# Depthwise causal convolution before a gated MLP: tokens at block edges from a ninth block of each unit, in place of products across blocks

## The chip, the cores and the metric

The kernel runs on one core of a Trainium2 chip. The metric is the device time of one execution in microseconds (us). The kernel before took 734.95 us, the median of three runs (734.82 to 735.59).

The core's engines are named as the profile names them: PE (matrix products, with its weight loads listed apart as PEld), DVE (vector), ACT (scalar and table functions), POOL (general) and SP (here it only issues DMAs and small order-keeping instructions).

## The reference, cut to what matters

`x` is 8 sequences of 4096 tokens with 192 channels in float32. The channels are 8 heads of 24, and each head has 7 taps, made a probability by a softmax:

```python
w = softmax(weight)                                # (8 heads, 7 taps)
y[b, s] = sum over k of w[h, k] * x[b, s + k - 6]  # per head, zeros before a sequence's start
h = y.reshape(32768, 192) @ w_in                   # (192, 2048)
out = (h * cos(h)) @ w_out                         # (2048, 192), float32
```

An output token thus needs itself and the six tokens before it.

## The kernel before, in words

**Units, blocks and tiles.** Tokens are cut into 32 units of 1024, a unit into 8 blocks of 128 tokens with the token on the partition. The MLP works on 64 tiles of 512 tokens, two to a unit.

**The convolution of a unit.** `load_unit` (L66) brings `x` in float32 on SP's queue. `cast_unit` (L163) turns it to bf16 on POOL in three instructions (L176 to L178), which also swap the two row halves of every odd head, and L172 copies the last block of the unit before into a slot ahead of block 0. `conv_mm` (L183) multiplies a block of one head by a banded 128x128 matrix of the taps (`band`); a second banded matrix (`prev`) brings in the last six tokens of the block before. Each product is done on one half of PE's rows (64 of 128), so that two products run side by side. `conv_part` (L210) does four heads: 12 products of 64 rows by 192 columns, six in the step called c1 and six in the step c2. Its two PSUM banks are then cast to bf16 by two ACT copies (`conv_out`, L201, the step called ec). A unit takes two such parts, one in each tile.

**Turning.** `double_unit` (L244, POOL) writes each 64-wide piece twice, and `turn_unit` (L250) sends the unit through a DMA transpose to `cT`, with channels on the partitions.

**The MLP.** A step h0 to h7 (`mm1`, L328) is six products of 64 rows by 512 columns into a PSUM tile `h`. ACT then takes the cosine (L334, as a sine) and DVE multiplies it with `h` to give `g` (L338); the multiply is the last reader of `h`. `h` has three buffers, taken in turn; in a tile the convolution's part takes one too, so the order is h0, conv, h1, h2, ... h7, and h2 gets the buffer of h0. A step "m8" (`mm2_step`, L358) is eight steps of two products of 64 rows by 192 columns, for the tiles before. `evac` (L370, ACT) takes its sums out of PSUM, `store` (L373) writes them.

**What sets the order.** It is written out by hand, once for PE and once for ACT:

```python
PE_ORDER = "h0 c1 m8 c2 h1 m8 h2 h3 m16 | h4 h5 m8 h6 m12 h7 m12"
ACT_ORDER = "P s0 ec s1 s2 s3 Q s4 s5 s6 s7"
PE_FIRST = ["h0 h1 h2 h3 h4 d1 h5 d2 h6 c1 h7 c2 |", "h0 m8 h1 m8 h2 h3 m16 | h4 c1 h5 m8 c2 h6 m12 h7 m12"]
```

s0 to s7 are the sines of h0 to h7 (each with DVE's multiply after it), P and Q the two `evac` copies. At h1 of even tiles POOL is given `double_unit`; at "|" SP is given the transpose (even tiles), the store and the next load (odd tiles), and POOL the cast of the unit after next (even tiles). Tiles 0 and 1 have orders of their own, and tile 0 does two parts (d1, d2 and c1, c2). Tiles 61 to 63 have no convolution, since unit 31 is the last.

`Turn` (L147) makes an empty instruction on SP wait for a product and a later product wait for SP, so that two row halves don't write one bank at a time. Such instructions stand in SP's queue between the DMAs.

Unit 0 is done ahead of the loop by `conv_first` (L278), on all 128 rows and with `prev` products, and turned in part by PE itself (`turn_first`, L288).

Of the kernel before, what the change touches and what calls it, by code (L numbers as in the profile page):

```python
# [8 lines left out]
FP32 = mybir.dt.float32  # L9
BF16 = mybir.dt.bfloat16  # L10
# [6 lines left out]
def kernel(  # L17
# [8 lines left out]
    nc = tc.nc  # L26
    B, S, D = x.shape
    H, K = weight.shape
    Dff = moe_w_in.shape[1]
    G = D // H  # L30
# [4 lines left out]
    U = 1024  # L35
    NU = NTOK // U
    UB = U // 128
    UPS = S // U
# [3 lines left out]
    NC = D // 64  # L42
    R = G // NC

    xf = x.rearrange("b s d -> (b s) d")

    consts = ctx.enter_context(tc.tile_pool(name="consts", bufs=1))
    xin = ctx.enter_context(tc.tile_pool(name="xin", bufs=2))
# [14 lines left out]

    x_tiles = {}

    def load_unit(u, n0=0, n1=UB):  # L66
        if n0 == 0:
            x_tiles[u] = xin.tile([128, UB, D], FP32, name="x_f")
        nc.sync.dma_start(out=x_tiles[u][:, n0:n1, :],
                          in_=xf[u * U + n0 * 128 : u * U + n1 * 128, :].rearrange("(n p) d -> p n d", p=128))  # L70

# [14 lines left out]
    def load_wo(q):  # L86
        for i in range(2):
            nc.sync.dma_start(out=wo_f[:, q * HP : (q + 1) * HP, i], in_=wo_src[:, q * HP : (q + 1) * HP, i])

    load_wo(0)  # L90


# [22 lines left out]
    E = 32 + K - 1  # L115
# [44 lines left out]

    bf = {}

    def cast_unit(u, n0=0, n1=UB):  # L163
        copy = nc.scalar.copy if u == 0 and n0 == 0 else nc.gpsimd.tensor_copy
        if u == 0:
            bf[u] = xb0
        else:
            bf[u] = xbf_pool.tile([128, UB + 1, D], BF16, name="x_bf")
            if u % UPS == 0:
                nc.gpsimd.memset(bf[u][:, 0, :], 0.0)  # L170
            else:
                nc.gpsimd.tensor_copy(out=bf[u][:, 0, :], in_=bf[u - 1][:, UB, :])  # L172

        o = bf[u][:, n0 + 1 : n1 + 1, :].rearrange("p n (h t k r) -> t p (n h) k r", t=2, k=NC, r=R)
        i = x_tiles[u][:, n0:n1, :].rearrange("p n (h t r k) -> t p (n h) k r", t=2, k=NC, r=R)
        copy(out=o[0], in_=i[0])  # L176
        copy(out=o[1, 0:64], in_=i[1, 64:128])  # L177
        copy(out=o[1, 64:128], in_=i[1, 0:64])  # L178
        bf.pop(u - 2, None)

    ct_tiles = {}

    def conv_mm(u, c, ps, i, rows, prev, n0, n1, **flags):  # L183

        h = 4 * c + i
        return nc.tensor.matmul(  # L186
            out=ps[i // 2][:, 0 : (n1 - n0) * 2 * G].rearrange("p (n k i r) -> p i n k r", n=n1 - n0, k=NC, i=2)[:, i % 2],
            lhsT=band[rows, h, 128 if prev else 0 : 256 if prev else 128],
            rhs=bf[u][rows, n0 + 1 - prev : n1 + 1 - prev, h * G : (h + 1) * G].rearrange("p n (k r) -> p n k r", k=NC),
            skip_group_check=True, **flags)  # L190

    def conv_out(u, c, ps, n0, m0, m1, copy, double=False):

        for b in range(2):
            w0 = (2 * c + b) * 2 * R
            o = ct_tiles[u][:, m0:m1, :, :, w0 : w0 + 2 * R].rearrange("p n k t w -> p (n k) t w")
            i = ps[b][:, (m0 - n0) * 2 * G : (m1 - n0) * 2 * G].rearrange("p (m t w) -> p m t w", t=1, w=2 * R)
            if double:
                copy(o, i.to_broadcast([128, (m1 - m0) * NC, 2, 2 * R]))  # L199
            else:  # L200
                copy(o[:, :, 0, :], i[:, :, 0, :])  # L201
# [8 lines left out]
    def conv_part(u, c, banks):  # L210


        ps = banks()
        sides = [slice(0, 64), slice(64, 128)]

        def mm(i, rows, prev=0, **flags):
            return conv_mm(u, c, ps, i, sides[rows], prev, 0, UB, **{"start": False, "stop": False, **flags})


        mm(0, 0, start=True)  # L220
        mm(2, 1, start=True)
        mm(1, 0)
        mm(2, 1, 1)
        m = mm(1, 0, 1)
        turn = Turn()
        turn.mark(m, mm(3, 1))
        yield
        m = mm(2, 0)
        turn.wait(m, mm(0, 1))
        mm(3, 0)  # L230
        mm(0, 1, 1)
        mm(3, 0, 1, stop=True)
        mm(1, 1, stop=True)
        yield
        if c == 0 and u not in ct_tiles:
            ct_tiles[u] = ct_pool.tile([128, UB, NC, 2, 64], BF16, name="ct")
        conv_out(u, c, ps, 0, 0, UB, nc.scalar.copy)
        yield

    cT = {}  # L240

    def double_unit(u, n0=0, n1=UB):
        ct = ct_tiles[u]
        nc.gpsimd.tensor_copy(out=ct[:, n0:n1, :, 1, :], in_=ct[:, n0:n1, :, 0, :])  # L244

    def turn_unit(u, n0=0, n1=UB):
        ct = ct_tiles.pop(u)
        if u not in cT:
            cT[u] = cT_pool.tile([128, UB, NC, 128], BF16, name="cT")
        nc.sync.dma_start_transpose(out=cT[u][:, n0:n1].rearrange("p n c k -> p (n c) k"),  # L250
                                    in_=ct[:, n0:n1].rearrange("p n c t k -> p (n c t k)"))
        cT.pop(u - 2, None)


    cast_unit(0, 0, NB)
# [4 lines left out]
    for d, n, m in ((0, 3, 3), (0, 1, 1), (2, 1, 4), (0, 1, 2)):  # L260
        nc.vector.tensor_tensor(out=prod[:, d : d + n], in0=prod[:, d : d + n], in1=prod[:, d + m : d + m + n], op=ALU.add)


    three = [nc.vector.tensor_copy, nc.scalar.copy, nc.gpsimd.tensor_copy]
    for odd in range(2):
        for q in range(4):
            e0 = 32 * (q ^ (2 * odd))
            three[(4 * odd + q) % 3](out=band[32 * q : 32 * q + 32, odd:H:2, e0 : e0 + E],
                                     in_=prod[32 * q : 32 * q + 32, 0, odd:H:2, :])
    cast_unit(0, NB, UB)  # L270
    for k in range(NC):
        three[(k + 2) % 3](out=w[:, k, 0:HP], in_=w_f[:, k, 0:HP])

    ct_tiles[0] = ct_pool.tile([128, UB, NC, 2, 64], BF16, name="ct")
    cT[0] = cT_pool.tile([128, UB, NC, 128], BF16, name="cT")
    copies = [nc.scalar.copy, nc.vector.tensor_copy]

    def conv_first(n0, n1):  # L278
        for c in range(2):
            ps = ring_banks()  # L280
            for i in range(4):
                for prev in range(2):
                    conv_mm(0, c, ps, i, slice(0, 128), prev, n0, n1, start=prev == 0 and i % 2 == 0, stop=prev == 1)
            yield
            for half in range(2):
                conv_out(0, c, ps, n0, n0 + 2 * half, n0 + 2 * half + 2, copies[half], double=n0 == 0)
# [25 lines left out]
    for q in range(2):  # L312
        nc.gpsimd.tensor_copy(out=wo[:, q * HP : (q + 1) * HP], in_=wo_f[:, q * HP : (q + 1) * HP])  # L313
    load_unit(2)


    g_tiles = {}
# [68 lines left out]
    for t in range(NT + 2):  # L386
        u, second = divmod(t, TPU)
        cu, cc = (u + 2, 0) if second else (u + 1, 1)
        conv = {"c": conv_part(cu, cc, ring_banks if t else o_banks) if cu < NU else iter(())}
        if t == 0:  # L390
            conv["d"] = conv_part(1, 0, o_banks)
        act, done, h, step = (ACT_ORDER if t > 1 else ACT_FIRST[t]).split(), set(), {}, 0

        def flush():
            while act:
                k = act[0]
                need = {"P": "start", "Q": "|", "e": k[1:] + "2"}.get(k[0], "h" + k[1:])
                if need not in done:
                    return
                act.pop(0)  # L400
                if k == "P" and 0 <= t - 2 < NT:
                    evac(t - 2, 0)
                    if t == NT + 1:
                        store(t - 2, 0, 1)
                elif k == "Q" and 0 <= t - 2 < NT:
                    evac(t - 2, 1)
                elif k[0] == "e":
                    next(conv[k[1]], None)
                elif k[0] == "s" and t < NT:
                    gcu(t, int(k[1:]), h.pop(int(k[1:])))  # L410

        done.add("start")
        flush()
        for k in (PE_ORDER if t > 1 else PE_FIRST[t]).split():
            if k[0] == "h" and t < NT:
                h[int(k[1:])] = mm1(t, int(k[1:]))
            elif k[0] in conv:
                next(conv[k[0]], None)
            elif k[0] == "m":
                for q in range(step, step + int(k[1:])):  # L420
                    mm2_step(t, q)
                step += int(k[1:])
            done.add(k)
            flush()

            if k == ("|" if t == 0 else "h1") and second == 0 and cu < NU:
                double_unit(cu)
            if k == "|":
                if second == 0 and cu < NU:
                    turn_unit(cu)  # L430
                if 0 <= t - 2 < NT:
                    store(t - 2, 1 if t == NT + 1 else 0)
                if second == 1 and u + 3 < NU:
                    load_unit(u + 3)
                if second == 0 and u + 2 < NU:
                    cast_unit(u + 2)


# [28 lines left out]
```

## Time and profile before

| | |
|---|---|
| profiled execution | 734.92 us |
| its span, first to last instruction | 733.1 us, so 1.82 us lie around it |
| granted PE clock | 0.999 |
| PE busy | 723.0 us, 99% |
| PEld busy | 554.6 us, 76% |
| DVE busy | 620.0 us, 85% |
| ACT busy | 626.9 us, 86% |
| POOL busy | 177.5 us, 24% |
| the convolution's 64-row products (L186, 192 columns) | 744, 243 ns each as recorded |
| the multiply (L338) | 512, 1221 ns each |
| the sine (L334) | 512, 1025 ns each |

The profile lists instructions by line, engine and shape, with their mean time. A product's recorded time contains its way through PE, so products overlap and their sum is no time of PE; what PE needs for a step is read from the distance between the starts of steps. The chain of waits goes back from the last instruction; each of its pieces is followed to what released it, or to the instruction before it on the same engine.

### The profile page before, as it was taken

To read this page: it belongs to the slowest core of one execution; us is meant where nothing else is said; L and a number is where in the kernel's file an instruction comes from. 1 tells how busy PE (TensorE), PEld (TensorE's weight loads), DVE (VectorE), ACT (ScalarE), POOL (GpSimd) and SP (SyncE) were. 2 spreads that over 40 slices of the span, in tenths; PEclk is the share of its full clock that TensorE was granted. 3 is DMA by queue.
4 is the path that set the end of the run, shared out by engine and by line. 5 is a ranking of instruction groups with operands and counts; after the bars stand their busy time and mean duration, and the time that the engine had idled before them with its cause. 6 is when DMAs were issued, how large, how long until landed. Compare 5 with 4: busy or idle time off the path is not lost.

```text
span 733.1 us, 26791 instructions
## 1 busy us (share of the span) xinstructions
PE 723.0 (99%) x12083; PEld 554.6 (76%) x12083; DVE 620.0 (85%) x538; ACT 626.9 (86%) x785; POOL 177.5 (24%) x177
## 2 busy tenths in 40 slices
PE   7899999999999999999999999999999999999997
PEld 3577777777777777777777777777777777777776
DVE  6888888888888888888888888888888888888883
ACT  6888888888888988988888888888888888888883
POOL 5522211222211222211222211222201222202000
PEclk9999999999999999999999999999999999999999
DMA  9624424434335455334334334344334355353302
GB/s 223 187 68 131 109 89 131 106 92 132 105 92 132 97 100 131 99 99 131 92 105 132 92 106 131 87 111 131 86 112 132 82 116 116 93 120 88 86 27 66
DMA packets 167956, 79.97 MB, mean 109 GB/s; under 512 B 99490, under 2 KB 167074, under 8 KB 167842
## 3 DMA queue, kind: packets, MB, share of 16 engines
q1 hardware_dynamic: 167840, 78.26, 40.8%
q8 instruction: 94, 1.54, 0.9%
q14 instruction: 20, 0.16, 0.1%
q10 hardware_dynamic: 2, 0.00, 0.0%
HBM read 28.31 MB, written 25.17 MB: 73 GB/s over the span
## 4 chain that ended last, share of the span: by engine, by line
PE 98%; DVE 1%; ACT 1%; issue 0%
PE o_ps L358 46%; PE h L328 45%; PE h L186 4%; PE o_ps L101 1%; PE h L358 1%; DVE g L338 1%; ACT cs L334 0%; ACT ct L201 0%; PE o_ps L186 0%; DVE cT L296 0%; ACT o_sb L370 0%; PE h L292 0%; PE o_ps L108 0%; ACT ct L199 0%; DVE ct L199 0%
## 5 line engine op out<-in xcount | busy, mean ns | idle before, releaser
L338 DVE TENSOR_TENSOR g<-h,cs 128x1024 bf16<-128x1024 f32 x512 | 609.1, 1221 | 97.4 <-ACT cs L334 88.8
L334 ACT ACTIVATE cs<-h 128x1024 bf16<-128x1024 f32 x512 | 511.5, 1025 | 78.4 <-PE h L328 77.1
L358 PEld LDWEIGHTS <-g 64*128 64x128 bf16 x8192 | 362.0, 94 | 67.8 <-issue 1.2
L328 PE MATMUL h<-cT,w 64*128 64x512 bf16 x3072 | 401.3, 376 | 2.7 <-DVE g L338 1.4
L358 PE MATMUL o_ps<-wo,g 64*128 64x192 bf16 x8064 | 403.3, 243 | 0.6 <-ACT ct L201 0.6
L328 PEld LDWEIGHTS <-w 64*128 64x128 bf16 x3072 | 166.1, 94 | 84.9 <-issue 3.0
L244 POOL COPY ct<-ct 128x1536 bf16<-128x1536 bf16 (+1 forms) x32 | 46.2, 1444 | 493.1 <-issue 489.6
L370 ACT COPY o_sb<-o_ps 128x384 f32<-128x384 f32 x126 | 60.4, 479 | 5.1 <-PE o_ps L358 2.4
L201 ACT CAST ct<-h 128x384 bf16<-128x384 f32 (+1 forms) x124 | 52.4, 474 | 9.5 <-PE h L186 5.5
L186 PE MATMUL h<-x_bf,band 64*128 64x192 bf16 (+1 forms) x752 | 53.4, 241 | 0.8 <-POOL x_bf L178 0.6
L186 PEld LDWEIGHTS <-band 64*128 64x128 bf16 (+1 forms) x776 | 38.2, 94 | 14.9 <-issue 1.3
L177 POOL CAST x_bf<-x_f 64x768 bf16<-64x768 f32 (+1 forms) x32 | 38.7, 1208 | 2.0
L178 POOL CAST x_bf<-x_f 64x768 bf16<-64x768 f32 (+1 forms) x32 | 38.6, 1206 | 1.9
L176 POOL CAST x_bf<-x_f 128x768 bf16<-128x768 f32 (+1 forms) x32 | 38.8, 1213 | 0.1
L101 PE MATMUL o_ps<-zero 128*128 128x512 bf16 x29 | 9.3, 489 | 1.3 <-DVE zero L96 1.3
L358 PE MATMUL h<-wo,g 64*128 64x192 bf16 x128 | 8.7, 243 | 0.6 <-ACT o_sb L370 0.6
L172 POOL COPY x_bf<-x_bf 128x192 bf16<-128x192 bf16 x24 | 8.3, 344 | 0.0
L101 PEld LDWEIGHTS <-zero 128*128 128x128 bf16 x29 | 3.2, 118 | 6.1 <-issue 3.0
L370 ACT COPY o_sb<-h 128x384 f32<-128x384 f32 x2 | 1.0, 480 | 5.2 <-PE h L358 5.2
L313 POOL CAST wo<-wo_f 128x1536 bf16<-128x1536 f32 x2 | 2.9, 1466 | 0.9 <-DMA wo_f<-in_moe_w_out_dram 0.8
L186 PE MATMUL o_ps<-x_bf,band 64*128 64x192 bf16 x24 | 2.1, 243 | 0.5 <-ACT ct L201 0.3
L258 DVE TENSOR_TENSOR prod<-mask,wn 128x2128 bf16<-128x2128 bf16 x1 | 2.4, 2376 | 0.1
(45 smaller groups left out, 29.3 us busy)
## 6 DMA issues: line engine op xcount, KB each, us to landing
out_dram<-o_sb SPq DMA_DIRECT2D x63, 384.0 KB, 2.9
x_f<-in_x_dram SPq DMA_DIRECT2D x31, 768.0 KB, 5.2
w_f<-in_moe_w_in_dram SPq DMA_DIRECT2D x4, 384.0 KB, 7.8
wo_f<-in_moe_w_out_dram SPq DMA_DIRECT2D x4, 384.0 KB, 4.9
x_f<-in_x_dram SPq DMA_DIRECT2D x2, 384.0 KB, 4.0
cT<-ct SPq DMA_TRANSPOSE x32, 4.6
out_dram<-o_sb SPq DMA_DIRECT2D x2, 192.0 KB, 1.9
w_row<-in_weight_dram ACTq DMA_DIRECT2D x1, 0.2 KB
```

The lines of the kernel that those rows point to most:

```text
L101: nc.tensor.matmul(out=idle, lhsT=zero[:, 0:128], rhs=zero, start=True, stop=True)
L176: copy(out=o[0], in_=i[0])
L177: copy(out=o[1, 0:64], in_=i[1, 64:128])
L178: copy(out=o[1, 64:128], in_=i[1, 0:64])
L186: return nc.tensor.matmul(out=ps[i // 2][:, 0 : (n1 - n0) * 2 * G].rearrange("p (n k i r) -> p i n k r", n=n1 - n0, k=NC, i=2)[:, i % 2], ...
L201: copy(o[:, :, 0, :], i[:, :, 0, :])
L244: nc.gpsimd.tensor_copy(out=ct[:, n0:n1, :, 1, :], in_=ct[:, n0:n1, :, 0, :])
L328: nc.tensor.matmul(out=h[:, i, :], lhsT=w[rows, k, j, :], rhs=c[rows, n0 : n0 + NB, k, :], start=(k == 0), stop=(k == NC - 1))
L334: nc.scalar.activation(out=cs, in_=h, func=AF.Sin, bias=math.pi / 2.0, scale=1.0)
L338: nc.vector.tensor_tensor(out=g_tiles[t][:, 2 * j : 2 * j + 2, :], in0=h, in1=cs, op=ALU.mult)
L358: m = nc.tensor.matmul(out=o_ps[tt, b][:, si * D : (si + 1) * D], lhsT=g_tiles[tt][rows, f, s * 128 : (s + 1) * 128], rhs=wo[rows, f // 2, ...
L370: nc.scalar.copy(o_sb[t][:, 2 * b : 2 * b + 2, :].rearrange("p s d -> p (s d)"), o_ps.pop((t, b))[:, 0 : 2 * D])
```

## The change

Each unit gets a ninth block. `load_edges` fetches, for each of the 8 blocks, the 16 tokens from 8 before the block's first to 7 after it (128 rows of 768 bytes). This block is cast, multiplied, doubled and turned with the other eight. Its tokens 8 to 13 of each group of 16 are the first six tokens of a block, and their whole history lies within the group. `mend_edges` then copies those over the first six tokens of each block in `cT`. So no product across blocks is needed, and with it go the swap of row halves in the cast and in `band`, the slot ahead of block 0 and its copy. `conv_part` has 8 products of 216 columns, where it had 12 of 192. Unit 0 keeps its form, apart from the swap.

```diff
+    def load_edges(u):
+        nc.sync.dma_start(out=x_tiles[u][:, UB, :],
+                          in_=xf[u * U - 8 : u * U - 8 + U, :].rearrange("(n t) d -> n t d", t=128)[:, 0:16, :])
...
-            x_tiles[u] = xin.tile([128, UB, D], FP32, name="x_f")
+            x_tiles[u] = xin.tile([128, UB + 1, D], FP32, name="x_f")
...
+    load_edges(1)
     load_wo(0)
...
-            if u % UPS == 0:
-                nc.gpsimd.memset(bf[u][:, 0, :], 0.0)
-            else:
-                nc.gpsimd.tensor_copy(out=bf[u][:, 0, :], in_=bf[u - 1][:, UB, :])
...
-        copy(out=o[0], in_=i[0])
-        copy(out=o[1, 0:64], in_=i[1, 64:128])
-        copy(out=o[1, 64:128], in_=i[1, 0:64])
+        o = 1 if u == 0 else 0
+        copy(out=bf[u][:, n0 + o : n1 + o, :].rearrange("p n (h k r) -> p (n h) k r", k=NC, r=R),
+             in_=x_tiles[u][:, n0:n1, :].rearrange("p n (h r k) -> p (n h) k r", k=NC, r=R))
+        if u and u % UPS == 0:
+            nc.gpsimd.memset(bf[u][0:8, UB, :], 0.0)
...
         mm(0, 0, start=True)
         mm(2, 1, start=True)
-        mm(1, 0)
-        mm(2, 1, 1)
-        m = mm(1, 0, 1)
         turn = Turn()
-        turn.mark(m, mm(3, 1))
+        turn.mark(mm(1, 0), mm(3, 1))
         yield
-        m = mm(2, 0)
-        turn.wait(m, mm(0, 1))
-        mm(3, 0)
-        mm(0, 1, 1)
-        mm(3, 0, 1, stop=True)
+        turn.wait(mm(2, 0), mm(0, 1))
+        mm(3, 0, stop=True)
         mm(1, 1, stop=True)
         yield
...
-        conv_out(u, c, ps, 0, 0, UB, nc.scalar.copy)
+        conv_out(u, c, ps, 0, 0, UB + 1, nc.scalar.copy)
...
-    def double_unit(u, n0=0, n1=UB):
+    def double_unit(u, n0=0, n1=UB + 1):
...
-    def turn_unit(u, n0=0, n1=UB):
+    def turn_unit(u, n0=0, n1=UB + 1):
...
+    def mend_edges(u):
+
+        nc.gpsimd.tensor_copy(out=cT[u][:, 0:UB, :, 0 : K - 1],
+                              in_=cT[u][:, UB].rearrange("p c (n t) -> p n c t", t=16)[:, :, :, 8 : 8 + K - 1])
...
-    for odd in range(2):
-        for q in range(4):
-            e0 = 32 * (q ^ (2 * odd))
-            three[(4 * odd + q) % 3](out=band[32 * q : 32 * q + 32, odd:H:2, e0 : e0 + E],
-                                     in_=prod[32 * q : 32 * q + 32, 0, odd:H:2, :])
+    for q in range(4):
+        three[q % 3](out=band[32 * q : 32 * q + 32, :, 32 * q : 32 * q + E], in_=prod[32 * q : 32 * q + 32, 0])
...
     load_unit(2)
+    load_edges(2)
...
                 if second == 1 and u + 3 < NU:
                     load_unit(u + 3)
+                    load_edges(u + 3)
                 if second == 0 and u + 2 < NU:
                     cast_unit(u + 2)
+                if second == 0 and cu < NU:
+                    mend_edges(cu)
```

In the instruction order of the changed kernel, each POOL round is `double_unit`, one cast of 128x1728, the mend. The first product of h0 in an even tile now also waits for POOL (the mend).

More of the change, by code (lines that the diff above doesn't have):

```diff
@@ L161, with cast_unit, conv_mm @@
     bf = {}
-    def cast_unit(u, n0=0, n1=UB):
+    def cast_unit(u, n0=0, n1=UB + 1):
         copy = nc.scalar.copy if u == 0 and n0 == 0 else nc.gpsimd.tensor_copy
-        if u == 0:
-            bf[u] = xb0
-        else:
-            bf[u] = xbf_pool.tile([128, UB + 1, D], BF16, name="x_bf")
-            if u % UPS == 0:
-                nc.gpsimd.memset(bf[u][:, 0, :], 0.0)
-            else:
-                nc.gpsimd.tensor_copy(out=bf[u][:, 0, :], in_=bf[u - 1][:, UB, :])
-        o = bf[u][:, n0 + 1 : n1 + 1, :].rearrange("p n (h t k r) -> t p (n h) k r", t=2, k=NC, r=R)
-        i = x_tiles[u][:, n0:n1, :].rearrange("p n (h t r k) -> t p (n h) k r", t=2, k=NC, r=R)
-        copy(out=o[0], in_=i[0])
-        copy(out=o[1, 0:64], in_=i[1, 64:128])
-        copy(out=o[1, 64:128], in_=i[1, 0:64])
+        bf[u] = xb0 if u == 0 else xbf_pool.tile([128, UB + 1, D], BF16, name="x_bf")
+        o = 1 if u == 0 else 0
[3 more added lines that the diff above has]
+            nc.gpsimd.memset(bf[u][0:8, UB, :], 0.0)
         bf.pop(u - 2, None)
     ct_tiles = {}
-    def conv_mm(u, c, ps, i, rows, prev, n0, n1, **flags):
+    def conv_mm(u, c, ps, i, rows, n0, n1, prev=0, **flags):
         h = 4 * c + i
@@ L188, in conv_mm @@
             lhsT=band[rows, h, 128 if prev else 0 : 256 if prev else 128],
-            rhs=bf[u][rows, n0 + 1 - prev : n1 + 1 - prev, h * G : (h + 1) * G].rearrange("p n (k r) -> p n k r", k=NC),
+            rhs=bf[u][rows, n0:n1, h * G : (h + 1) * G].rearrange("p n (k r) -> p n k r", k=NC),
             skip_group_check=True, **flags)
@@ L214, in conv_part, with mm @@
         sides = [slice(0, 64), slice(64, 128)]
-        def mm(i, rows, prev=0, **flags):
-            return conv_mm(u, c, ps, i, sides[rows], prev, 0, UB, **{"start": False, "stop": False, **flags})
+        def mm(i, rows, **flags):
+            return conv_mm(u, c, ps, i, sides[rows], 0, UB + 1, **{"start": False, "stop": False, **flags})
         mm(0, 0, start=True)
         mm(2, 1, start=True)
-        mm(1, 0)
-        mm(2, 1, 1)
-        m = mm(1, 0, 1)
         turn = Turn()
-        turn.mark(m, mm(3, 1))
+        turn.mark(mm(1, 0), mm(3, 1))
         yield
-        m = mm(2, 0)
-        turn.wait(m, mm(0, 1))
-        mm(3, 0)
-        mm(0, 1, 1)
-        mm(3, 0, 1, stop=True)
+        turn.wait(mm(2, 0), mm(0, 1))
+        mm(3, 0, stop=True)
         mm(1, 1, stop=True)
@@ L235, in conv_part @@
         if c == 0 and u not in ct_tiles:
-            ct_tiles[u] = ct_pool.tile([128, UB, NC, 2, 64], BF16, name="ct")
-        conv_out(u, c, ps, 0, 0, UB, nc.scalar.copy)
+            ct_tiles[u] = ct_pool.tile([128, UB + 1, NC, 2, 64], BF16, name="ct")
+        conv_out(u, c, ps, 0, 0, UB + 1, nc.scalar.copy)
         yield
     cT = {}
-    def double_unit(u, n0=0, n1=UB):
+    def double_unit(u, n0=0, n1=UB + 1):
         ct = ct_tiles[u]
         nc.gpsimd.tensor_copy(out=ct[:, n0:n1, :, 1, :], in_=ct[:, n0:n1, :, 0, :])
-    def turn_unit(u, n0=0, n1=UB):
+    def turn_unit(u, n0=0, n1=UB + 1):
         ct = ct_tiles.pop(u)
         if u not in cT:
-            cT[u] = cT_pool.tile([128, UB, NC, 128], BF16, name="cT")
+            cT[u] = cT_pool.tile([128, UB + 1, NC, 128], BF16, name="cT")
         nc.sync.dma_start_transpose(out=cT[u][:, n0:n1].rearrange("p n c k -> p (n c) k"),
@@ L272 @@
         three[(k + 2) % 3](out=w[:, k, 0:HP], in_=w_f[:, k, 0:HP])
-    ct_tiles[0] = ct_pool.tile([128, UB, NC, 2, 64], BF16, name="ct")
-    cT[0] = cT_pool.tile([128, UB, NC, 128], BF16, name="cT")
+    ct_tiles[0] = ct_pool.tile([128, UB + 1, NC, 2, 64], BF16, name="ct")
+    cT[0] = cT_pool.tile([128, UB + 1, NC, 128], BF16, name="cT")
     copies = [nc.scalar.copy, nc.vector.tensor_copy]
@@ L282, in conv_first @@
                 for prev in range(2):
-                    conv_mm(0, c, ps, i, slice(0, 128), prev, n0, n1, start=prev == 0 and i % 2 == 0, stop=prev == 1)
+                    conv_mm(0, c, ps, i, slice(0, 128), n0 + 1 - prev, n1 + 1 - prev, prev, start=prev == 0 and i % 2 == 0, stop=prev == 1)
             yield
```

## The prediction

> **What bounds the kernel now.** The page says PE: 99% busy, and 98% of the chain that ended last. Read alone, this makes each product removed a gain. But a recorded product contains its way through PE, and the chain names PE wherever it finds an earlier product. So I went on to the chain in order of time, for one tile (tile 31; a piece is a step of the written order):
>
> ```profile
> 357.53 0.65 PE h L328 x6
> 358.18 0.25 PE h L186 x6
> 358.42 0.66 PE o_ps L358 x16
> 359.08 0.25 PE h L186 x6
> 359.33 0.65 PE h L328 x6
> 359.98 0.66 PE o_ps L358 x16
> 360.64 1.38 PE h L328 x12
> 362.02 1.32 PE o_ps L358 x32
> 363.34 1.30 PE h L328 x12
> ```
>
> In order: h0, c1, m8, c2, h1, m8, h2 with h3, m16, h4 with h5. Columns are start, length, what. The reader should compare the two pieces "x12": h4 and h5 take 1.30 us, h2 and h3, the same work, 1.38. So 0.08 of waiting hides at h2, which the waits list does not show. The timeline of the three engines says for what:
>
> ```profile
> 358.21 1.02 ACT L334 ACTIVATE cs<-h 128x1024 bf16<-128x1024 f32 x1 [0.15 <-PE h L328]
> 359.27 1.23 DVE L338 TENSOR_TENSOR g<-h,cs 128x1024 bf16<-128x1024 f32 x1 [0.41 <-ACT cs L334]
> 359.41 0.86 ACT L201 CAST ct<-h 128x384 bf16<-128x384 f32 x2 [0.17 <-PE h L186]
> 360.16 1.04 ACT L334 ACTIVATE cs<-h 128x1024 bf16<-128x1024 f32 x1
> 360.55 1.47 PE L328 MATMUL h<-cT,w 64*128 64x512 bf16 x12
> ```
>
> h0's sine starts when h0 is done, the multiply when the sine is done (359.27), it ends at 360.50, and h2 starts at 360.55. h2 takes the buffer of h0, which that multiply frees. In the instruction starts of the trace this holds in every tile from 2 to 60: h2 begins 0.053 or 0.054 us after the end of g0, and 3.196 to 3.200 after h0's start. PE's own work in between, by the lengths of pairs worked out next, is h0 and h1 0.647 each, c1 and c2 0.248 each, two m8 of 0.66: 3.11. So it is the path h0, sine, multiply, h2 that sets this stretch, 0.09 longer than the work; the tile's other 7.84 us (period 11.04) run without a gap. c1 and c2, all that the change shortens on PE, lie in the stretch that already waits.
>
> **PE.** A pair of 192-column products takes 1.32 us / 16 = 0.0825 us (the piece x32), a pair of 512 takes 1.30 / 6 = 0.216, so a column costs 0.000417 us and a pair of 216 columns 0.0925. A part had 6 pairs, 0.495 us, and gets 4, 0.37: 0.125 less, in 62 parts 7.75 us. In tiles 2 to 60 h2 still starts 3.20 after h0. The work before it becomes 2.98, the wait 0.215, the gain 0. What is late next is that same multiply.
>
> A rule bears on this. The Trainium skill, "Perfetto Trace Analysis", section "Identifying the Most-Contended Engine", says that the busy share of matmuls is a bad measure of how near PE is to its limit, and to take MFU or the busy share of weight loads. By its measure (here 76%) PE has room, by the 99% it has none and the sum would be the whole 7.75; the gap at h2 agrees with the rule, but what the change is worth comes from the gap, not from either share.
>
> **Tiles without convolution** look like counter-evidence. Tiles 61 and 62 are 10.57 apart, 0.47 less than 11.04. But there the convolution takes no buffer of `h`, h2 gets that of the tile before's h7, and it starts 0.42 before the end of g0. The change keeps the buffer.
>
> **ACT.** The two ec copies grow from 384 to 432 columns. The page's casts from PSUM by L201 take 242 ns at 96 and 482 at 384: 0.83 ns a column, 0.04 us more each. c2 ends 0.125 earlier, so ec starts that much earlier (ACT is free then: s0 ends 1.888 after h0, ec would start at 1.894). s1 moves by -0.125 + 0.08, a little earlier, and s2 waits for h2 as before. The tightest place behind it: in odd tiles g1 ends 0.007 before g2 starts, and h5 starts 0.064 beyond the 0.053 that it needs after g2. So the two copies may grow by 0.125 + 0.07, about 0.10 each, before a tile gets longer. Other buffers: h1 starts 0.29 after the multiply that frees its own, and moving 0.125 earlier leaves 0.17, over 0.053.
>
> **POOL.** The copy L244 grows from 1536 to 1728 columns, with 825 ns at 768 and 1464 at 1536 by 0.16. The casts (0.34 and three of 1.23) become one of 1728: 702 ns at 384 and 1230 at 768 give 1.38 ns a column, so 2.55, some 1.5 less a round. The mend (128 rows, 24 runs of 6) has no row. From below 0, from above the 1.46 of the copy of 1536; I take 0.34, the copy of 192. It waits for the transpose, whose landing (4.6, with 27/24 of the blocks 5.2) falls about 11.3 after its tile's h0; the mend is done by 11.7, and its reader, h0 of the next even tile, comes at 22.08. Even at 1.46, 9 us are left. Behind it in POOL's queue stands the next copy L244, 25 after this h0. All hidden.
>
> **SP and DMA.** The transpose occupies SP 3.09 us, with 27/24 3.48: the store behind it ends about 0.39 later, and the next order-keeping instruction comes 0.97 after that. The edge load is one issue every two tiles, behind the load of x. Its nearest row is that load, 0.50 us; from above the start-up's wo load, 1.83. The next such instruction is 3.8 us away. It lands some 5.2 us after issue; its cast starts 8 after. Hidden; without the cover (edges over 2.8 us later) the cast slips, and it has 4 us and more before the next tile's c1. A further wait at h0 in even tiles is on a transpose and a multiply that ended long before (the latter 0.95 us): nothing.
>
> **Start-up.** Band copies and casts of unit 0 get shorter, but PE runs its warming products until 11.0 us while the last band copy ends at 10.0. POOL's later cast held back one group (0.28), but the next group waits for DVE's copies anyway, which wait on the first group. In tile 1, c1 waited for POOL until 31.98; this looks like a gain, but the chain goes past it:
>
> ```profile
> 28.90 1.03 ACT cs L334
> 29.93 0.02 issue
> 29.95 2.37 DVE g L338 x2
> 32.32 0.04 issue
> 32.36 0.82 PE h L328 x6
> ```
>
> h5 waits for g3, not for c1. What moves: in tile 0 the ACT copies of both parts are on the path (tile 0's second part waits for the first one's copies, tile 1's m8 for the second's): +0.08 of copies less 0.04 of products, then +0.04, so +0.08 for h5; then c2 gives back 0.06. Sum +0.02. Bounds: all of it hidden and c2 kept, -0.1; an edge load or POOL in the way for one round, +0.6.
>
> **Sum.** 733.1 + 59 x 0 + 0.02 = 733.12, with the 1.82 around it 734.94 for the profiled execution's 734.92, which lies 0.03 below the median of the runs. Forecast 734.9 us: no change. What a measurement of this kernel can tell from none is about 0.2%, 1.5 us. Its own range is 734.6 to 735.6.
>
> **Rivals.**
>
> *PE is the bound after all.* Then the 62 parts give 62 x 0.125 = 7.75, and the time is 727.2. For: 99%, the chain's 98%, and the end tiles' 10.57. Against: the 0.053 after g0 in all 59 tiles. It would need the sine or the multiply to be shorter or h2 another buffer; nothing does that. 7 in 100, with a part of it.
>
> *The widened ec copies become the wait.* They stand in ACT's queue ahead of s1; from +0.10 us each they delay g1, g2 and so h5 in every tile. If the nine-block copy from PSUM costs 0.15 more each, s1 is 0.175 late, h5 about 0.1, and 59 x 0.1 = 6 us: 741. For: the slack of 0.07 is small, and 60 tiles repeat it. Against: 0.83 ns a column would have to be over 2. 8 in 100, smaller losses over 1.5 us included.
>
> *The change doesn't do what it says*: PE does not get shorter, since 8 products need 8 loads of weights of 94 ns. Weight loads run beside products (a pair in 0.0825 with two loads), and the time would be the same as in the forecast; it counts there.
>
> **Chances.** No change 0.85, faster by over 0.2% 0.07, slower by over 0.2% 0.08. The range 734.2 to 736.2 is the forecast's, with the start-up's bounds and some of the smaller losses; under 2 in 10 lie outside.
>
> **What would show it.** Right: period 11.04, h2 still 3.20 after h0 and 0.05 after g0, with a piece h2 and h3 of 1.5 in the chain; c1 and c2 at 0.185 each; ec copies near 0.52; POOL less busy by about 1 us a round. Wrong: a period under 11.0 (the first rival); a gap at h5 with s1 later than before (the second); h0 of even tiles waiting for POOL (the mend); c1 of odd tiles waiting for POOL (the edge load).

## The result, and the profile after

| | before | after |
|---|---|---|
| time, median of 4 runs each on one chip | 735.27 us | 734.73 us (734.26 to 735.56) |
| ratio | | 0.9994, 95% interval 0.9977 to 1.0012 |
| profiled execution, its span | 734.92, 733.1 us | 735.56, 733.8 us |
| period of tiles 2 to 60 | 11.04 us | 11.04 us |

No difference can be told. (The kernel before has 735.27 here and 734.95 further up because a fourth run, 735.58, came to the three.) Yet the change does what it says: it took a third of the tile's convolution products out. The busy shares and the counts of the changed kernel's page, and then four of its groups by shape (count, busy us, mean ns of one, idle time before them):

```profile
PE 720.5 (98%) x11835; PEld 546.5 (74%) x11835; DVE 619.8 (84%) x537; ACT 630.4 (86%) x781; POOL 150.0 (20%) x119
```

```profile
L174 POOL CAST x_bf<-x_f 128x1728 bf16<-128x1728 f32 x31 | 79.4, 2562 | 0.0
...
L200 ACT CAST ct<-h 128x432 bf16<-128x432 f32 x120 | 56.4, 522 | 1.6
L236 POOL COPY ct<-ct 128x1728 bf16<-128x1728 bf16 x31 | 50.5, 1630 | 374.2 <-ACT ct L200 374.2
...
L248 POOL COPY cT<-cT 128x144 bf16<-128x144 bf16 x31 | 9.6, 309 | 153.7 <-DMA cT<-ct 69.3 <-PE o_ps L352 58.1 <-PE h L185 23.8
```

There are 248 products fewer (4 in each of 62 parts). The ec copy (L200) takes 522 ns (482 before), the one cast of a unit (L174) 2.56 us in place of four instructions, the mend (L248) 0.31 us. PE's busy time fell by only 2.5 us. A product is recorded for 243 ns while the next one starts long before that, so a wait after it lies mostly inside its record: the last product ahead of h2 ends, as recorded, 0.03 before h2 starts, though the wait there is 0.21. The chain in order of time, for the same tile 31 as before (start, length, what):

```profile
357.87 0.65 PE h L322 x6
358.52 0.18 PE h L185 x4
358.70 0.66 PE o_ps L352 x16
359.36 0.18 PE h L185 x4
359.55 0.65 PE h L322 x6
360.20 0.66 PE o_ps L352 x16
360.86 0.04 issue
360.89 1.47 PE h L322 x12
362.36 1.32 PE o_ps L352 x32
363.68 1.29 PE h L322 x12
```

c1 and c2 are 0.18 each (0.25 before), and what they gave up stands at h2: its piece x12 is 1.47, and a piece "issue" now lies ahead of it. By the instruction starts, h2 follows the start of the product before it by 0.276 us (0.151 in the kernel before; 0.063 at h4, where there is no wait), so the wait is 0.21 us. The timeline says again for what:

```profile
358.56 1.02 ACT L328 ACTIVATE cs<-h 128x1024 bf16<-128x1024 f32 x1 [0.15 <-PE h L322]
...
359.61 1.23 DVE L332 TENSOR_TENSOR g<-h,cs 128x1024 bf16<-128x1024 f32 x1 [0.41 <-ACT cs L328]
359.63 0.94 ACT L200 CAST ct<-h 128x432 bf16<-128x432 f32 x2
```

The multiply ends at 360.84 and h2 starts at 360.89. In every tile from 2 to 60 h2 still starts 3.196 to 3.200 after h0 and 0.053 or 0.054 after g0.

The profiled execution's span is 0.64 longer than before's. The 59 tiles have 0.00 of it. The first convolution product came 0.28 later (PE's warming products took longer, see the last section), the rest of the start-up added 0.06, and the end behind the last products 0.30 (see the account of the prediction).

### The profile page after: what moved, and what is told of

Read it like the earlier page. It is cut to its first block, busy times and chain, and to the rows that moved or that the text cites. A ratio compares the mean times of both kernels' runs of the same rounds, so it can differ in the third digit from the quotient of the medians.

```text
span 733.8 us, 26364 instructions
## 1 busy us (share of the span) xinstructions
PE 720.5 (98%) x11835; PEld 546.5 (74%) x11835; DVE 619.8 (84%) x537; ACT 630.4 (86%) x781; POOL 150.0 (20%) x119
## 4 chain that ended last, share of the span: by engine, by line
PE 97%; DVE 1%; ACT 1%; issue 1%
PE h L322 46%; PE o_ps L352 46%; PE h L185 3%; PE o_ps L107 1%; DVE g L332 1%; PE h L352 1%; ACT cs L328 0%; ACT ct L200 0%; ACT ct L198 0%; DVE cT L289 0%; ACT o_sb L364 0%; PE h L285 0%; PE o_ps L114 0%; PE o_ps L185 0%; DVE zero L102 0%
## 5 line engine op out<-in xcount | busy, mean ns | idle before, releaser
L236 POOL COPY ct<-ct 128x1728 bf16<-128x1728 bf16 (+1 forms) x32 | 51.4, 1605 | 377.3 <-ACT ct L200 374.2
L174 POOL CAST x_bf<-x_f 128x1728 bf16<-128x1728 f32 (+1 forms) x32 | 80.7, 2521 | 0.1
L200 ACT CAST ct<-h 128x432 bf16<-128x432 f32 (+1 forms) x124 | 57.2, 513 | 2.2 <-PE h L185 0.6
L185 PE MATMUL h<-x_bf,band 64*128 64x216 bf16 (+1 forms) x512 | 45.5, 250 | 0.7 <-ACT ct L200 0.7
L248 POOL COPY cT<-cT 128x144 bf16<-128x144 bf16 x31 | 9.6, 309 | 153.7 <-DMA cT<-ct 69.3
L185 PEld LDWEIGHTS <-band 64*128 64x128 bf16 (+1 forms) x528 | 27.9, 94 | 15.1 <-issue 1.0
L185 PE MATMUL o_ps<-x_bf,band 64*128 64x216 bf16 x16 | 1.7, 252 | 0.6 <-ACT ct L200 0.6
```

Source lines behind the costliest of these rows:

```text
L174: copy(out=bf[u][:, n0 + o : n1 + o, :].rearrange("p n (h k r) -> p (n h) k r", k=NC, r=R), in_=x_tiles[u][:, n0:n1, :].rearrange("p n (h ...
L185: return nc.tensor.matmul(out=ps[i // 2][:, 0 : (n1 - n0) * 2 * G].rearrange("p (n k i r) -> p i n k r", n=n1 - n0, k=NC, i=2)[:, i % 2], ...
L248: nc.gpsimd.tensor_copy(out=cT[u][:, 0:UB, :, 0 : K - 1], in_=cT[u][:, UB].rearrange("p c (n t) -> p n c t", t=16)[:, :, :, 8 : 8 + K - 1])
```

## The experiments

All ratios are to the kernel before on the same chip. "Period" is the distance from the h0 of tile 2 to that of tile 61, divided by 59.

### Less work on PE alone, in the kernel before

The products across blocks are left out of `conv_part`, and nothing is put in their place.

```diff
-        mm(1, 0)
-        mm(2, 1, 1)
-        m = mm(1, 0, 1)
+        m = mm(1, 0)
...
-        mm(3, 0)
-        mm(0, 1, 1)
-        mm(3, 0, 1, stop=True)
+        mm(3, 0, stop=True)
```

> The kernel before, with the products across blocks left out (so the first six tokens of each block lack their history from the block before) and nothing of the change added: 8 products of 192 columns a part in place of 12, 2 pairs of 0.0825 us less, 0.165 a part and 10.2 us in 62 parts. Theory (in tiles 2 to 60 h2 waits for the multiply that frees h0's buffer): the period stays 11.04, the wait before h2 grows from 0.09 to 0.25, the time stays within 0.5 us of the kernel before. Rival one (PE's work sets the time, and the change's new parts ate the gain): 10.2 us less, 724.7. Rival two (the change's own additions cost something that balanced a real gain): the same 724.7.

Measured: 734.72 us (734.70 to 735.06), ratio 0.9996 (0.9987 to 1.0005), period 11.040. Its chain in the same tile:

```profile
357.64 0.66 PE h L324 x6
358.30 0.02 issue
358.32 1.03 ACT cs L330
359.36 0.02 issue
359.38 1.24 DVE g L334
360.62 0.04 issue
360.66 1.47 PE h L324 x12
```

With nothing added, PE's saving is still worth nothing, so no added copy or DMA ate it. The chain no longer passes through c1, m8 and c2: it goes from h0 through the sine and the multiply to h2, as the prediction said.

### A shorter path, in both kernels

Tile 2 onwards, the sine s0 is made for half the columns and its multiply reads it twice. The path h0, s0, g0, h2 gets shorter by half a sine.

```diff
-        nc.scalar.activation(out=cs, in_=h, func=AF.Sin, bias=math.pi / 2.0, scale=1.0)
+        short = j == 0 and t > 1
+        if short:
+            nc.scalar.activation(out=cs[:, 0, :], in_=h[:, 0, :], func=AF.Sin, bias=math.pi / 2.0, scale=1.0)
+        else:
+            nc.scalar.activation(out=cs, in_=h, func=AF.Sin, bias=math.pi / 2.0, scale=1.0)
...
+                                in1=cs[:, 0:1, :].to_broadcast([128, 2, T]) if short else cs, op=ALU.mult)
```

In the kernel before:

> The kernel before, where from tile 2 on the first sine of a tile, s0, is taken over half the columns, and the multiply g0 uses that half for both halves of h0 (so half the cosines of h0 are not its own). PE's and DVE's work is unchanged; ACT has some 0.43 us less a tile. Theory: the path h0, s0, g0, h2 gets 0.43 shorter, the wait of 0.09 before h2 goes, the next limit (g1, g2, then h5) allows 0.08 to 0.09 a tile: 59 x 0.085 = 5.0 us less, about 730. Rival (PE's work sets the period): no change. Rival (ACT's total sets the period): 59 x 0.43 = 25 us less.

In the changed kernel:

> The changed kernel with the same shortened s0 (half the cosines of h0 are not its own). Theory: the wait before h2 is 0.215 here, so the same edit gives more than on the kernel before: g1 and g2 then allow 0.125 in odd and 0.17 in even tiles, 59 x 0.15 = 8.7 us less than the changed kernel, about 726; 3.7 us of it are what the change had saved on PE and could not show. Rival (the change saves nothing on PE, or its additions ate it): the same gain as on the kernel before, 5.0 us, about 730.

Measured: 729.85 us before (729.78 to 730.23; ratio 0.993, 0.9915 to 0.9945) and 722.22 changed (721.82 to 722.75; ratio 0.9826, 0.9811 to 0.984). Periods 10.955 and 10.830. Two pieces of the changed kernel's chain, h2 with h3 among them:

```profile
353.69 0.66 PE o_ps L357 x16
354.34 1.30 PE h L322 x12
```

The piece x12 is back at 1.30: no wait is left at h2, which starts 2.985 after h0 (3.110 in the kernel before, PE's own work in each). The two kernels now lie 7.6 us apart, and 59 tiles by the 0.125 of the prediction are 7.4. The saving on PE was real and is paid as soon as the wait is gone. My expectation of 726 for the changed kernel missed by 4: I let h5 wait for g2 (h5 takes the buffer that g2, the multiply of h2, frees), with multiplies one behind the other by their recorded 1.22. In the starts of the trace they follow each other every 1.14, so g2 ends just in time for h5.

### Filling the wait with other work

In the changed kernel, m8 before h2 becomes m9 and m16 behind h3 m15. The same in the kernel before.

```diff
-    PE_ORDER = "h0 c1 m8 c2 h1 m8 h2 h3 m16 | h4 h5 m8 h6 m12 h7 m12"
+    PE_ORDER = "h0 c1 m8 c2 h1 m9 h2 h3 m15 | h4 h5 m8 h6 m12 h7 m12"
```

> The changed kernel with one of the 64 steps of the second product moved from behind h3 to before h2 (m9 and m15 for m8 and m16), nothing left out. Theory: PE waits before h2 with or without this step, so the step is done in the wait and h4 and h5 come earlier by 0.0825, until h5 meets the multiply g2 (0.064 beyond what it needs): period 10.976, 59 x 0.064 = 3.8 us less, 731. Rival (PE's work sets the period): the order of PE's steps makes no difference. Rival (DVE or ACT totals set it): no difference.

> The kernel before with one step moved before h2 (m9 and m15), nothing left out. Theory: its wait of 0.09 before h2 takes the step of 0.0825 as well, and h5 then meets g2 at the same place, so the period is the same 10.97 as on the changed kernel, 731: the 4 us of that run belong to the order and not to the change. Rival (the room before h2 is the change's alone): no gain, 735.

Measured: 730.96 us changed (730.55 to 731.5; ratio 0.9946, 0.993 to 0.9963) and 731.07 before (730.91 to 731.64; ratio 0.9946, 0.9934 to 0.9959), periods 10.972 and 10.974. In the changed kernel h2 still starts 3.198 after h0 and h5 now waits for g2 (0.053 behind its end). The step moved is 0.0825 long, and 0.068 of it was gained. The kernel before gains as much, so this gain belongs to the order, none of it to the change.

### A path cut in two halves, in both kernels (expectation wrong)

s0 and g0 are each done in two halves of 512 columns, so that the first half's multiply could begin under the second half's sine.

```diff
+        parts = ((0, 1), (1, 2)) if j == 0 and t > 1 else ((0, 2),)
+        for i0, i1 in parts:
+            nc.scalar.activation(out=cs[:, i0:i1, :], in_=h[:, i0:i1, :], func=AF.Sin, bias=math.pi / 2.0, scale=1.0)
+        for i0, i1 in parts:
+            nc.vector.tensor_tensor(out=g_tiles[t][:, 2 * j + i0 : 2 * j + i1, :], in0=h[:, i0:i1, :], in1=cs[:, i0:i1, :], op=ALU.mult)
```

In the changed kernel:

> The changed kernel with s0 and g0 of every tile from 2 on done in two halves of 512 columns, nothing left out. The first half's multiply can start when half the sine is done (a sine of 512 columns took 0.597 us in the run with the shortened s0, where g0 began 1.496 after h0), so the second half's multiply should end some 2.8 after h0 in place of 3.145, and h2 finds its buffer free before PE comes to it at 2.985. Theory: period 10.83, PE's own work, as in the run with the shortened s0, 722 us, 1.8 per cent below the kernel before; ACT and DVE have more work a tile (0.17 and 0.16) and it costs nothing. Rival (ACT's or DVE's total sets the period, since they are given more): 735 or over. Rival (the shortened s0 gained by taking work from ACT, not by the wait): no gain here, 735.

In the kernel before:

> The kernel before with the same split of s0 and g0, nothing left out. Theory: the wait of 0.09 before h2 goes, period 10.955, 729.9 us; the distance to the changed kernel with the split, 59 x 0.125 = 7.4 us, is what the change saves on PE once nothing else sets the stretch. Rival (the change's saving is not real or its additions cost something): the two kernels with the split are equally fast.

Measured: 742.60 us (742.07 to 743.1; ratio 1.0102, 1.0086 to 1.0117) and 742.68 (742.58 to 743.33; ratio 1.0105, 1.009 to 1.012). The timeline of the changed kernel with halves:

```profile
361.18 1.08 ACT L333 ACTIVATE cs<-h 128x512 bf16<-128x512 f32 x2
...
362.30 1.29 DVE L335 TENSOR_TENSOR g<-h,cs 128x512 bf16<-128x512 f32 x2 [0.47 <-ACT cs L333]
```

The first multiply starts (362.30) when both half sines are done (362.26), not after one. In the trace only the second half sine updates the semaphore that DVE's first half multiply waits for, so the halves cannot overlap in this program. Two half sines take 1.08 against 1.03 for a whole, two half multiplies 1.30 against 1.23, so the path to the end of g0 is 0.113 longer and h2 starts 3.316 after h0 (3.198 without the halves). A miss as a way to shorten the path, but the cleanest sign of what sets the period: with the longer path both kernels have the same period, 11.172, though PE's work differs by 0.125 a tile. The rival that ACT's or DVE's total sets the period had asked for 735 or over, which came too. But here ACT is 85% busy and DVE 84%, no more than in the kernel before (86% and 85%), and h2 again starts right behind the multiply, 0.058 to 0.059 after its end in every tile.

### The cover of the mend

The mend is done ten times.

```diff
-        nc.gpsimd.tensor_copy(out=cT[u][:, 0:UB, :, 0 : K - 1],
+        for _ in range(10):
+            nc.gpsimd.tensor_copy(out=cT[u][:, 0:UB, :, 0 : K - 1],
```

> The changed kernel with the mend (POOL, 0.31 us in its profile) done ten times in place of once, with the same result: 2.8 us more on POOL in every second tile, in POOL's queue ahead of the next doubling, and ahead of h0 of the next even tile, which waits for the last mend. Theory (hidden, some 10 us of cover): no change, 734.7 to 735.5. Rival (the additions on POOL are what balanced a gain): about 31 x 2.8 = 87 us more, or a part of it.

Measured: 734.95 us (734.22 to 735.53), ratio 0.9998 (0.9989 to 1.0007). POOL's timeline:

```profile
358.79 3.63 POOL L249 COPY cT<-cT 128x144 bf16<-128x144 bf16 x10 [5.87 <-PE h L185]
370.86 1.63 POOL L236 COPY ct<-ct 128x1728 bf16<-128x1728 bf16 x1 [8.44 <-ACT ct L200]
```

3.3 us more on POOL cost nothing. The ten copies end at 362.42, and 8.44 us of idle time are left before POOL's next copy.

### The margin of the ec copies

The changed kernel repeats the second ec copy of a part (from unit 2 on), to the same place: one more instruction in ACT's queue ahead of s1.

```diff
-    def conv_out(u, c, ps, n0, m0, m1, copy, double=False):
+    def conv_out(u, c, ps, n0, m0, m1, copy, double=False, banks=(0, 1)):
...
-        for b in range(2):
+        for b in banks:
...
         conv_out(u, c, ps, 0, 0, UB + 1, nc.scalar.copy)
+        if u > 1:
+            conv_out(u, c, ps, 0, 0, UB + 1, nc.scalar.copy, banks=(1,))
```

> The changed kernel with ec of units from 2 on made longer by a third copy (the second bank is cast once more to the same place, 0.41 us more on ACT ahead of s1), the results unchanged. It tests the rival that the widened copies become the wait. ACT stays below its time (86 per cent busy and some 4 more). Theory by the corrected distance of multiplies that follow each other (1.14 us from start to start, as the short-s0 run shows, not their duration 1.22): s1 0.41 later, g2 ends 6.6 after h0, h5 comes 0.15 to 0.20 late in each tile, 59 x 0.18 = 10.5 us more, 745. By the margin that the prediction gave (0.07 beyond the 0.045 that s1 had gained): h5 0.24 to 0.30 late, 16 us more, 751. Rival (only totals count): no change, 735.

Measured: 752.88 us (752.65 to 753.91), ratio 1.024 (1.0223 to 1.0257), period 11.352. The chain of one tile, from the copies on:

```profile
368.63 0.95 ACT ct L200 x2
...
370.02 1.04 ACT cs L330
...
371.08 2.37 DVE g L334 x2
...
373.49 0.82 PE h L324 x6
```

The second rival's mechanism exists: ec copies, s1, g1 and g2 in a row, h5. The expected 745 was too short because the third copy put s1 off by 0.56, more than the 0.415 between the starts of the first two, because it waits for the end of the copy to the same place (0.555 behind it). h5 came 0.34 (odd tiles) and 0.29 (even) late, so the room before h5 was 0.22 to 0.27. Multiplies 1.14 apart give h5's place to within 0.01; by the prediction's 1.22 h5 would have come 0.08 later still. The copies had grown by 2 x 0.04 already, so from the kernel before's they could have grown by 0.22 + 0.08 = 0.30 together, 0.15 each, where the prediction had 0.10.

### An order made for the path, in both kernels

Steps of m are moved into the stretches that wait, and Q goes ahead of s3.

```diff
-    PE_ORDER = "h0 c1 m8 c2 h1 m8 h2 h3 m16 | h4 h5 m8 h6 m12 h7 m12"
-    ACT_ORDER = "P s0 ec s1 s2 s3 Q s4 s5 s6 s7"
+    PE_ORDER = "h0 c1 m8 c2 m5 h1 m5 h2 m14 | h3 h4 m5 h5 m12 h6 m5 h7 m10"
+    ACT_ORDER = "P s0 ec s1 s2 Q s3 s4 s5 s6 s7"
```

In the changed kernel:

> The changed kernel with another written order, nothing left out: PE does h0 c1 m8 c2 m5 h1 m5 h2 m14 | h3 h4 m5 h5 m12 h6 m5 h7 m10, and ACT does Q after s2 in place of after s3. Two steps more stand before h2 and five steps of the second half before h5, so that the waits before h2 and h5 are filled. Worked out from the measured lengths (sine 1.024 and 0.92 from start to start, multiply 1.22 and 1.14 from start to start, a step of the second product 0.0825): period 10.92, 59 x 0.12 = 7.1 us less than the kernel before, 727.8. Rival (the stretch is set by something else than the waits before h2 and h5): a period of 10.97 or more, 731 or over.

In the kernel before:

> The kernel before with the same order. Its c1 and c2 are 0.125 longer a tile, and the order leaves no room for them: by the same lengths the period is 11.04, 735.2. The distance to the changed kernel with this order, 7.4 us, is then the change's saving, in two kernels that compute all of the reference. Rival (the change saves nothing): both equally fast.

Measured: 726.62 us changed (725.97 to 726.9), ratio 0.9883 (0.987 to 0.9897), period 10.896; 734.02 before (733.88 to 734.65), ratio 0.9987 (0.9977 to 0.9996), period 11.021. Of the changed kernel's chain, from c1 to h2:

```profile
353.40 0.25 PE h L185 x4
...
354.31 0.18 PE h L185 x4
...
355.97 0.65 PE h L322 x6
```

h2 (the last line, six products alone) is 0.65, without a gap. A new wait of 0.06 stands at c1 (0.25 where c2 takes 0.18), for a multiply of the tile before. This version computes everything and beats both kernels, by 1.2% (1.0 to 1.3%). Both times came 1.2 us below what was expected. Under this order the change is worth 734.02 - 726.62 = 7.4 us, PE's whole saving.

## Why the prediction was right

**The wait at h2.** It was 0.215 as said, and the period did not move. Three tests show that the path sets it: with PE's work alone reduced the period stays (11.040), with the path shortened the two kernels part by 7.6 us, with the path lengthened both have the same period.

**PE.** The saving of 0.125 a part holds: c1 and c2 at 0.18 each, and 7.6 and 7.4 us between the kernels where the wait is gone. The 7.75 of the first rival was the right size of the saving, at the wrong place. The busy share of weight loads (76% before, 74% after) did not tell the two apart; the gap at h2 did.

**ACT.** The copies grew by 0.040 each, as worked out. s1 starts 0.045 earlier after h0 than before, which is -0.125 + 0.08. The margin of 0.10 for each copy was too small (about 0.15 by the third-copy run), since it stacked recorded multiplies of 1.22 us that follow each other at 1.14. The second rival is a real mechanism, further off than said.

**POOL.** Cast 2.56 (2.55 said), the wide copy 1.63 (1.62), the mend 0.31 (0.34). The mend starts 11.2 to 13.1 after its tile's h0, where 11.3 was said. In 16 of the 31 rounds it starts 5.0 to 5.4 after the issue of the transpose that it waits for, as scaled (5.2); in the other 15 it starts 6.6 to 6.9 after it (374.87 to 381.55 in one round), and why is not shown. Its reader comes at 22.08, so this costs nothing. POOL is 27.5 us less busy, 0.9 a round.

**SP.** The transpose mostly occupies SP 3.4 to 3.6 us (3.48 said), in six of 32 rounds 4.5 to 4.8; in the kernel before, too, six took 3.8 to 4.6. The edge load takes 0.65, above the row of 0.50 that I took; two of the 31, at 1.91 and 1.98, went beyond the bound of 1.83. None of this shows in the 59 tiles.

**Start-up.** In the two profiled executions compared above it was +0.06 where +0.02 was said. The copies' +0.08 is there; the 0.06 that c2 was to give back is not, since h7 of tile 1 waited as long for a multiply.

The prediction also put PE's wait for POOL's later cast of unit 0, which the change shortens, at nothing. That holds where the warming products end late, as in these two: PE waited 0.28 us there in the kernel before. In the profile of the kernel before with the last experiment's order the first convolution product came at 9.97 us instead of 11.00, and PE then waited 1.23 us for the same cast, so h0 of tile 0 still started at 15.25. The changed kernel with that order had its first product at 9.97 as well and started h0 at 14.73. So in some executions the change saves about half a microsecond here, a term that the sum did not have.

**The end.** The sum had no term for it either. From the end of the last copy to the end of the span there are 3.40 to 3.42 us in all seven profiles of the changed kernel and its variants, and 3.10 to 3.11 in all six of the kernel before and its variants. So the 0.30 comes with the change. It is a pause of 0.37 us on SP between two of the waits that close the program; in the kernel before the steps there are 0.03 to 0.05. Why SP pauses stays open. This cost and the saving at the start have opposite signs and are both too small for the measured times to tell; that they have opposite signs is luck, and no merit of the sum.

## What to carry to other kernels

A saving on the busiest engine is worth what it takes out of stretches which that engine sets; a stretch that begins with a buffer's fill and ends with its next use can be set by the way through the other engines. Look for it by comparing equal pieces of the chain (1.38 against 1.30 for the same twelve products), and test it by lengthening or shortening that way in both kernels. A change that gives nothing under one order can give its whole price under another, so after such a result move work into the new wait before the change is given up.

## What the runs showed of the hardware

**The same 29 warming products take 8.1 to 9.6 us.** They are PE's first work and read a tile of zeros; the code is the same in all kernels. The group in the kernel before and in the kernel before with m9:

```profile
L101 PE MATMUL o_ps<-zero 128*128 128x512 bf16 x29 | 9.3, 489 | 1.3 <-DVE zero L96 1.3
```

```profile
L101 PE MATMUL o_ps<-zero 128*128 128x512 bf16 x29 | 8.1, 440 | 1.3 <-DVE zero L96 1.3
```

The first convolution product starts between 9.8 and 11.3 us across the profiled executions. In the changed kernel and its variants h0 of tile 0 moves with it (14.47 to 15.66), about as far as the runs of that kernel spread (734.3 to 735.6). In the kernel before and its variants h0 moves less (15.23 to 15.58), because of the wait for POOL's cast told above. So a change of less than 1 us is not to be read from single executions here.

**Instructions of one engine overlap.** Multiplies recorded at 1.22 us follow each other every 1.14 where they wait for nothing else, copies from PSUM recorded at 0.52 every 0.415; but in the third-copy run the copy to the place of the one before came 0.555 after its start, behind its end. Chains over one engine are to be worked out with distances between starts.
